# A planned order of the matmul steps in a fused attention and GEGLU kernel

## The chip, the cores and the metric

The kernel runs on one NeuronCore of a Trainium2 chip. The metric is the device time of one execution in microseconds (us). A core has five engines with a queue each, worked off in order: TensorE (PE; its weight loads are shown as PEld), VectorE (DVE), ScalarE (ACT), GpSimd (POOL) and SyncE (SP), which here only issues DMAs. Matmuls write to eight banks of an accumulator memory, PSUM.

## The reference

The input x has 2048 rows of 576. After a layer norm, two branches are computed from the same rows and multiplied:

```python
xn = _layernorm(x)
# A: 32 heads of width 18
q, k, v = split(xn @ wqkv)
p = softmax(q @ k.T * 18 ** -0.5)
s = concat_heads(p @ v) @ wo
# B: gated MLP, inner width 4608
h = gelu(xn @ w_gate) * (xn @ w_up)
g = silu(h @ w_down)
out = x + s * g
```

All is fp32. The kernel gets near fp32 from fp16 matmuls by splitting operands into a high and a low half (three products for one).

## The kernel before, in words

**Stages.** A first stage (to about 210 us) makes the layer norm, the first projections and the row maxima of head pair 0. Then the main loop (lines 1464 to 1528) goes over head pairs 0 to 14, 64 steps each. A last stage (from line 1544) does pair 15, the output projection and the gating.

**A step of the main loop** issues, in this order: `qk2` (line 1265), the scores of this pair for one key tile, followed by the exponential on ScalarE (L1275, from PSUM tile s2); `qk1` (line 1212), scores of the next pair, followed by their row maxima on VectorE (L1220, from s1); and then one of three fillings. s1 and s2 exist once, so the next step's scores wait for this step's maximum and exponential. The fillings are:
- *gate slots* (`g_run`, line 1001): the GEGLU's first matmuls. `Pair` (line 415) computes a tile of the gate and one of the up product in banks ma and mb at once, with half the array each, in two stages of 14 and 13 slots (L443, two matmuls a slot). At the end of the second, ScalarE empties ma (gs, L608) and mb (gv, L619), and a chain follows on GpSimd (L631 to L634), ScalarE (tanh, L637), GpSimd (L644, L645), ScalarE (hhi, L659) and GpSimd (hlo, L666).
- *a down stage* (`DownPair.run`, line 716): half of a down product, in the two-bank tile md (L729). After the second one VectorE adds md to the sum y (L749, called late in the step).
- *a PV run* (`burst`, line 1300): probabilities by values for the two to four key tiles that are waiting, in one bank, in fp32 (L1310). VectorE then adds the bank to osb (L1316, L1318).

In before, a running account (`stored`) of the work left, spread over the steps left, says how many slots a step gets, and whether a down pair may begin. When a gate pair closes, the next step makes the PV run, in bank ma and, if anything is left, mb.

**Deferred work.** `subtick` (line 141) is called once in each step. It advances a clock of ticks: deferred functions (the chain of a gate pair, the division of finished heads) come due some ticks after they were asked for, if the step has room for them; the room is given to it by engine, in us (A for ScalarE, V for VectorE, T for the step's length, which pays back GpSimd). Behind them comes a background list, `bg`, of pieces that prepare the weights.

**Weights.** Chunks follow each other in the gate stream: projection chunks j1 to j4 (seven heads each) and gate chunks c0 to c17 (256 inner columns each), in the order j1, c0, c1, j2, c2, c3, j3, c4, c5, j4, c6 and so on to c17, then the output weights. `prep` (line 195) prepares one in pieces: load; absolute maxima on VectorE (L234, L239); exchange of the maximum through DRAM (L260, L275); a power-of-two scale (L281 to L298); five times a high half on ScalarE (L316) and a low half on GpSimd (L323, L324); the same for the down weights (L333). A VectorE piece asks for 0.7 of V, a ScalarE piece for 0.7 of A. When the gate stream comes to a chunk, `unit_w` (line 963) calls `until` (line 160), which repeats subticks, with plenty of room, till the last piece of that chunk is issued; then the chunk's first slot is issued.

**Finished heads.** `norm` (line 1323) divides by the row sums. The sums go through DRAM and back in four DMAs (a1, a2, b1, b2), since the reciprocal has to be spread over the rows of each head; the steps are chained by ticks. Only the last one of all (pair 15, second half) does it on VectorE with a shuffle and a reciprocal over all 512 columns (L1335, L1336).

Of the kernel before, what the change touches and what calls it, by code (L numbers as in the profile page):

```python
# [12 lines left out]
F32 = mybir.dt.float32  # L13
F16 = mybir.dt.float16
I32 = mybir.dt.int32
AF = mybir.ActivationFunctionType
# [4 lines left out]
P = 128  # L21
# [75 lines left out]
def kernel(ctx: ExitStack, tc: tile.TileContext, x, wqkv, wo, w_gate, w_up, w_down, out):  # L97
# [1225 lines left out]
    def norm(p, qh, o):  # L1323
        st = {}
        last = p == NPAIR - 1

        def a():
            if o is None:
                st["o"] = osum.pop((p, qh))
                return  # L1330
            st["o"] = ap.tile([P, 512], F32, tag="osb", name=f"osb_{p}_{qh}", bufs=2)
            nc.scalar.activation(st["o"], o, AF.Copy)
            if last and qh == 1:
                st["b"] = ap.tile([P, 512], F32, tag="obr", name=f"obr_{p}_{qh}", bufs=1)
                nc.vector.stream_shuffle(st["b"], st["o"], mask=[DH] * 32)  # L1335
                nc.vector.reciprocal(st["b"], st["b"])  # L1336
                return

        def a1():
            st["sd"] = dp.tile([4, 512], F32, tag="sd", name=f"sd_{p}_{qh}", bufs=2)  # L1340
# [54 lines left out]
            defer.at(defer.now + dt, run, cost)  # L1395

        a()
        if last and qh == 1:
            for fn in (c, d, e, g):
                fn()  # L1400
        else:
            dma = ((1, a1, None), (3, a2, None), (3, b, None), (1, b1, None), (2, b2, None))
            if p < NPAIR - 2:
                chained(*dma, (4, c, on_dve()), (1, d, on_act()), (1, e, on_dve()), (1, f, None))
            else:
                dma = ((1, a1, None), (2, a2, None), (2, b, None), (1, b1, None), (1, b2, None))

                def rest():
                    for fn in (c, d, e, g if last else f):
                        fn()  # L1410

                chained(*dma, (3, rest, on_dve()))
# [33 lines left out]
    zero_last()  # L1446
    pend = []
    dn = None
    stored = 0.0
    gs.closed = False  # L1450
    G_SLOT, D_STAGE = 0.2158, 0.735
    whole = (NPAIR - 1) * 4 * NT
    dleft = 2 * NCH * NT

    def flush(tags):

        for tag in tags:
            if not pend:
                return
            n = next((k + 1 for k, u in enumerate(pend) if u[2] == NT - 1), len(pend))  # L1460
            burst(pend[:n], tag)
            del pend[:n]

    for p in range(NPAIR - 1):
        if p not in VT:
            load_v(p)
        for i in range(4 * NT):
            s, half = divmod(i, 2)
            qh, kt = divmod(s, NT)
            if i == 0:  # L1470
                until(lambda: mdone.get(p))
            if i == 52 and p + 2 < NPAIR:
                load_qk(p + 2)
            kp = p + 1 if s < 30 else p + 2
            if i == 60:
                items = iter(range(64))
            pt = qk2(p, 2 * qh + half, kt, "s2")
            if half == 0:
                pa = pt
            else:  # L1480
                pend.append((p, qh, kt, pa, pt))
            if kp < NPAIR:
                qk1(kp, next(items))
            if i == 62:
                steps[2]()
            stored += (gs.left * G_SLOT + dleft * D_STAGE) / max(1, whole - 64 * p - i)
            late = False
            spent = 0.0
            held = 2 * len(pend) + (half == 0)
            cap = 8 if 64 * p + i < whole - 3 else 6  # L1490
            if dn is None and len(dnq) > 1 and not 58 <= i <= 60 and (gs.closed or held < cap - 2):
                dn = DownPair()
                dn.run()
                spent = D_STAGE
            elif dn is not None:
                late = dn.run()
                spent = D_STAGE
            if spent:
                dleft -= 1
            stored -= spent  # L1500
            if gs.closed:
                gs.closed = False
                if late:
                    dn.evac()
                    dn = None
                k = len(pend)
                subtick({"A": 2.2, "V": 1.4 if late else 2.2, "T": 1.0 + 0.86 * k})
                flush(("ma", "mb"))
            else:
                subtick({"A": 0.75, "V": 0.0 if late else 0.75, "T": 1.85})  # L1510
                if late:
                    dn.evac()
                    dn = None
                r = g_left()
                n = max(stored, (1.8 if late else 1.27) - spent) / G_SLOT
                if n < r:
                    n = math.ceil(r / max(1, round(r / max(n, 1.0))))
                n0 = gs.left
                g_run(n)
                stored -= (n0 - gs.left) * G_SLOT  # L1520
                if held >= cap and not gs.closed:
                    subtick({"A": 1.5, "V": 1.5, "T": 3.0})
                    flush(("md",))
            if i == 60:
                steps[1]()
            if i == 59:
                steps = max_end(p + 1)
                steps[0]()
# [97 lines left out]
```

## Time and profile before

| | us |
|---|---|
| median of 3 runs (lowest to highest) | 2699.47 (2698.98 to 2701.22) |
| the profiled execution's own time | 2701.04 |
| its span, first to last instruction | 2699.0 |

The profile has the span's busy times by engine, groups of instructions by source line (L1310 is line 1310), the waits by pair of engine and releaser, and a timeline. In the timeline a row is: start, busy time, engine, line, operation, output<-inputs, shapes, count, and in brackets the idle time of the engine before it with what ended it. TensorE's work overlaps its weight loads, and its ends are modelled.

### The profile page before, as it was taken

How to read it: one execution, taken by the hardware profiler on the slowest of the kernel's cores; microseconds unless marked ns; L12 is line 12 of the kernel's file. 1: busy time of each engine (PE TensorE's matmuls, PEld its weight loads, DVE VectorE, ACT ScalarE, POOL GpSimd, SP SyncE). 2: the span in 40 equal slices, each digit the busy share in tenths (PEclk: the TensorE clock that was granted, in tenths of full speed). 3: DMA queues.
4: the chain of work that ended last, by engine and by line, in shares of the span. 5: the costliest groups of instructions: out<-in, count | busy, mean ns of one | idle time of the engine just before them, and what ended most of it. 6: DMA issues, size and time to landing. Idle time of an engine off the chain costs nothing.

```text
span 2699.0 us, 59766 instructions
## 1 busy us (share of the span) xinstructions
PE 2556.7 (95%) x25292; PEld 1359.9 (50%) x25292; DVE 1922.6 (71%) x2718; ACT 1655.4 (61%) x2083; POOL 1485.3 (55%) x1422
## 2 busy tenths in 40 slices
PE   6979999999999999999999999999999999999898
PEld 5554545455545544445554545555455555544344
DVE  7677778777777787677767777777777777766534
ACT  5216666666667665666666666767666666666663
POOL 4236663575357553657575665747476675756201
PEclk9989999999999999999999999999999999999999
DMA  4420111201130022011111111111011120100033
GB/s 142 140 80 23 21 38 54 68 17 28 58 82 12 9 53 64 26 38 32 30 28 32 36 28 38 41 24 47 15 32 28 38 54 10 43 14 15 7 103 114
DMA packets 134068, 118.90 MB, mean 44 GB/s; under 512 B 60456, under 2 KB 113088, under 8 KB 133800
## 3 DMA queue, kind: packets, MB, share of 16 engines
q1 hardware_dynamic: 128168, 103.31, 14.7%
q0 software_dynamic: 3072, 8.90, 1.0%
q8 instruction: 197, 3.23, 0.5%
q10 hardware_dynamic: 2560, 2.89, 0.3%
q14 instruction: 71, 0.58, 0.1%
HBM read 85.16 MB, written 29.63 MB: 43 GB/s over the span
## 4 chain that ended last, share of the span: by engine, by line
PE 76%; DVE 11%; ACT 7%; issue 3%; DMA 2%; POOL 0%; SPq 0%; ACTq 0%; DVEq 0%
PE ma_t L443 15%; PE ma_t L1310 15%; PE md_t L729 13%; PE mb_t L443 13%; PE s L1269 7%; PE s L1217 6%; DVE PM L1220 3%; ACT P L1275 3%; ACT gs L608 2%; DVE osb L1318 2%; DVE y L749 2%; PE pv L1291 1%; PE mc_t L462 1%; PE mb_t L1310 1%; ACT hhi L659 1%
## 5 line engine op out<-in xcount | busy, mean ns | idle before, releaser
L1220 DVE TENSOR_REDUCE PM<-s 128x2 f32<-128x1024 f32 x1024 | 1251.5, 1223 | 349.6 <-PE s L1217 345.4
L1275 ACT ACTIVATE P<-s,etab 128x1024 f32<-128x1024 f32 x896 | 996.9, 1113 | 738.5 <-PE s L1269 728.4
L443 PE MATMUL ma_t<-XHT,whi_c 64*128 64x512 f16 x1440 | 541.2, 376 | 22.6 <-DVE osb L1318 18.9
L443 PE MATMUL mb_t<-XHT,whi_c 64*128 64x512 f16 x1440 | 542.0, 376 | 3.2 <-DVE touch L413 1.2
L443 PE MATMUL ma_t<-XHT,wlo_c 64*128 64x512 f16 x1296 | 487.0, 376 | 0.0
L1310 PE MATMUL ma_t<-P,VT 128*32 128x512 f32 x3624 | 421.6, 597 | 38.7 <-ACT gs L608 29.3
L443 PE MATMUL mb_t<-XL,whi_c 64*128 64x512 f16 x1152 | 433.0, 376 | 0.0
L443 PE MATMUL mb_t<-XHT,wlo_c 64*128 64x512 f16 x1152 | 432.9, 376 | 0.0
L443 PE MATMUL ma_t<-XL,whi_c 64*128 64x512 f16 x1152 | 432.9, 376 | 0.0
L1269 PE MATMUL s<-QT,KT 56*128 56x512 f16 x2048 | 408.2, 380 | 14.5 <-ACT P L1275 10.7
L443 PEld LDWEIGHTS <-whi_c 64*128 64x128 f16 x5184 | 289.6, 94 | 252.6 <-issue 51.8
L1217 PE MATMUL s<-KT,QT 54*128 54x512 f16 x2048 | 408.2, 379 | 5.9 <-DVE PM L1220 3.3
L644 POOL TENSOR_SCALAR tw<-tw 128x512 f32<-128x512 f32 x144 | 88.9, 618 | 522.2 <-ACT tw L637 522.2
L729 PE MATMUL md_t<-dhi_c,hhi 64*128 64x288 f16 x2264 | 340.6, 283 | 7.5 <-DVE touch L413 4.2
L729 PE MATMUL md_t<-dhi_c,hlo 64*128 64x288 f16 x2264 | 340.4, 282 | 0.0
L729 PE MATMUL md_t<-dlo_c,hhi 64*128 64x288 f16 x2264 | 339.9, 282 | 0.0
L729 PEld LDWEIGHTS <-hhi 64*128 64x128 f16 x4528 | 249.4, 94 | 138.9 <-issue 34.7
L666 POOL TENSOR_TENSOR hlo<-gv,hhi 128x512 f16<-128x512 f32 x144 | 168.6, 1171 | 198.9 <-ACT hhi L659 198.9
L1269 PEld LDWEIGHTS <-KT 56*128 56x128 f16 x2048 | 129.2, 94 | 281.7 <-issue 193.9
L1318 DVE TENSOR_TENSOR osb<-ma_t,osb 128x512 f32<-128x512 f32 x142 | 98.0, 690 | 209.3 <-PE ma_t L1310 209.3
L1310 PEld LDWEIGHTS ma_t<-P,VT 128*32 128x32 f32 x3624 | 103.1, 109 | 261.8 <-issue 190.7
L631 POOL TENSOR_TENSOR tw<-gs 128x512 f32<-128x512 f32 x144 | 150.1, 1043 | 120.0 <-ACT gs L608 119.2
(261 smaller groups left out, 4071.5 us busy)
## 6 DMA issues: line engine op xcount, KB each, us to landing
draw_c<-in_B_w_down SPq DMA_DIRECT2D x18, 576.0 KB
raw_c<-in_B_w_gate SPq DMA_DIRECT2D x18, 512.0 KB
raw_c<-in_B_w_up SPq DMA_DIRECT2D x18, 512.0 KB
obr<-rd SPq DMA_DIRECT2D x31, 256.0 KB
KT<-KD SPq DMA_DIRECT2D x32, 224.0 KB
QT<-QD SPq DMA_DIRECT2D x32, 216.0 KB
VS<-vst POOLq DMA_DIRECT2D x16, 304.0 KB, 3.8
VT<-VS SPq DMA_DIRECT2D x16, 304.0 KB
```

The lines of the kernel that those rows point to most:

```text
L443: nc.tensor.matmul(o, lw, xx, start=self.stage == 0 and self.k == 0, stop=self.stage == 1 and self.k == self.slots - 1, skip_group_check=True,
L608: nc.scalar.activation(st["g"], g.t, AF.Copy, scale=w.uE[:, 0:1])
L631: gp.tensor_tensor(st["t"], st["g"], st["g"], op=ALU.mult)
L644: gp.tensor_scalar(st["t"], st["t"], 1.0, 1.0, op0=ALU.mult, op1=ALU.add)
L666: gp.tensor_tensor(hs.lo[:, ft], st["v"], hs.hi[:, ft], op=ALU.subtract)
L729: nc.tensor.matmul(self.t.t[:, hf, 0:288], a[r, ft, sl], b[r, ft, 288 * hf:288 * hf + 288], start=self.stage == 0 and k == 0, stop=self.st ...
L1217: nc.tensor.matmul(s1[:, h], QT[p][r, P * qt:P * qt + P], KT[p][r, 512 * kb:512 * kb + 512], start=True, stop=True)
L1220: nc.vector.tensor_reduce(PM[p][:, :, qt, kb:kb + 1], s1, op=ALU.max, axis=AX.X)
L1269: nc.tensor.matmul(s2[:, h], KT[p][r, P * kt:P * kt + P], QT[p][r, 512 * qb:512 * qb + 512], start=True, stop=True)
L1275: nc.scalar.activation(pt, s2, AF.Exp, scale=ETAB[j0])
L1310: nc.tensor.matmul(t.t[qd:qd + 32, :], VT[p][:, c0:c0 + 32], pt[:, h], start=kt == k0, stop=kt == k1, skip_group_check=True,)
L1318: nc.vector.tensor_tensor(osum[p, qh], t.t, osum[p, qh], op=ALU.add)
```

## The change

- **A plan for each gate pair.** When a pair has closed and its PV run is issued, `make_plan` tries every pattern of the next 4 to 7 steps: which of them have a down stage, where the pair's first stage ends, and how the 14 and 13 slots are shared out (`spread`). The pattern with the least modelled loss (`lost`, which follows TensorE and the row maxima with fixed times) is taken, with small penalties for a length or a number of down stages off the average. The account `stored` is gone. The last step of a plan makes the PV run.
- **Room for VectorE.** In a step that isn't a run, V was 0.75 unless a down pair ended there. Now it is 0.75 only if also the step's planned work (0.735 for a down stage and 0.2158 a slot) is 2.0 or more. In a run step it stays 2.2 (1.4 where a down pair ends).
- **The run's bank.** With a down stage in the step, ma and mb as before; without one, md, and ma for a second run.
- **The end.** The plan spreads the work over the steps left and LEAD = 10 more, so that some gate slots and down pairs fall into the last stage. By the order of instructions, 40 slots do, and 18 single down products in place of 10.
- **One norm.** Pair 14's second half takes the way without DRAM, too.

```diff
--- before.py
+++ after.py
@@ -1324,17 +1324,18 @@
         st = {}
         last = p == NPAIR - 1
 
+        direct = qh == 1 and p >= NPAIR - 2
+
         def a():
             if o is None:
                 st["o"] = osum.pop((p, qh))
-                return
-            st["o"] = ap.tile([P, 512], F32, tag="osb", name=f"osb_{p}_{qh}", bufs=2)
-            nc.scalar.activation(st["o"], o, AF.Copy)
-            if last and qh == 1:
+            else:
+                st["o"] = ap.tile([P, 512], F32, tag="osb", name=f"osb_{p}_{qh}", bufs=2)
+                nc.scalar.activation(st["o"], o, AF.Copy)
+            if direct:
                 st["b"] = ap.tile([P, 512], F32, tag="obr", name=f"obr_{p}_{qh}", bufs=1)
                 nc.vector.stream_shuffle(st["b"], st["o"], mask=[DH] * 32)
                 nc.vector.reciprocal(st["b"], st["b"])
-                return
 
         def a1():
             st["sd"] = dp.tile([4, 512], F32, tag="sd", name=f"sd_{p}_{qh}", bufs=2)
@@ -1395,8 +1396,8 @@
             defer.at(defer.now + dt, run, cost)
 
         a()
-        if last and qh == 1:
-            for fn in (c, d, e, g):
+        if direct:
+            for fn in (c, d, e, g if last else f):
                 fn()
         else:
             dma = ((1, a1, None), (3, a2, None), (3, b, None), (1, b1, None), (2, b2, None))
@@ -1446,11 +1447,80 @@
     zero_last()
     pend = []
     dn = None
-    stored = 0.0
     gs.closed = False
-    G_SLOT, D_STAGE = 0.2158, 0.735
+    G_SLOT, D_STAGE, BLOCK, BURST = 0.2158, 0.735, 0.43, 2.9
+    ROW_MAX, EVAC, ADD, TOUCH = 1.28, 0.86, 0.75, 0.15
+    LEAD = 10
     whole = (NPAIR - 1) * 4 * NT
-    dleft = 2 * NCH * NT
+    dleft = [2 * NCH * NT]
+    plan = deque()
+    frac = [0.0, 0.0]
+
+    def spread(total, ds, lates):
+
+        n = len(ds)
+        base = (total * G_SLOT + sum(ds) * D_STAGE - 0.4 * sum(lates)) / n
+        left, out = total, []
+        for k in range(n):
+            w = base + 0.4 * lates[k] - ds[k] * D_STAGE
+            m = left if k == n - 1 else min(left, max(0, round(w / G_SLOT)))
+            out.append(m)
+            left -= m
+        return out
+
+    def lost(steps):
+
+        t = vec = red = 0.0
+        ideal = 0.0
+        for d, g, late, first in steps:
+            t1 = max(t + 0.21, red + 0.055)
+            e1 = t1 + 0.22
+            vec = red = max(vec, e1 + 0.16) + ROW_MAX - 0.05
+            w = d * D_STAGE + (BURST if g is None else g * G_SLOT)
+            if d:
+                vec = max(vec, e1 + D_STAGE) + (EVAC if late else TOUCH)
+            t = e1 + w
+            if g is None:
+                vec = max(vec, t) + ADD
+            elif first:
+                vec = max(vec, t) + TOUCH
+            ideal += BLOCK + w
+        return max(t, red + 0.055 - 0.21) - ideal
+
+    def make_plan(now, held, mid, avail):
+
+        pairs = max(1.0, gs.left / 27)
+        size = (whole + LEAD - now) / pairs + frac[0]
+        want = min(8.0, dleft[0] / pairs + frac[1])
+        best = None
+        for n in range(max(4, math.floor(size) - 1), min(9 - held, 7, math.ceil(size) + 1) + 1):
+            for bits in range(1 << n):
+                ds = [bits >> k & 1 for k in range(n)]
+                lates, run, ok, starts = [], mid, True, 0
+                if mid and not ds[0]:
+                    continue
+                for k, d in enumerate(ds):
+                    lates.append(bool(d and run))
+                    if d and not run:
+                        starts += 1
+                        at = now + k
+                        ok = ok and not 58 <= at % 64 <= 60 and at < whole - 1 and starts <= avail
+                    if run and not d:
+                        ok = False
+                    run = bool(d) and not run
+                if not ok:
+                    continue
+                for m in range(1, n - 1):
+                    gl = spread(14, ds[:m], lates[:m]) + spread(13, ds[m:n - 1], lates[m:n - 1]) + [None]
+                    seq = [(d, g, l, k == m - 1) for k, (d, g, l) in enumerate(zip(ds, gl, lates))]
+                    works = [d * D_STAGE + g * G_SLOT for d, g, _, _ in seq[:-1]]
+                    cost = lost(seq) + 0.3 * abs(n - size) + 0.15 * abs(sum(ds) - want) + 0.02 * (max(works) - min(works))
+                    if best is None or cost < best[0]:
+                        best = (cost, seq, works + [9.0])
+        _, seq, works = best
+        frac[0] = max(-1.5, min(1.5, size - len(seq)))
+        frac[1] = want - sum(d for d, _, _, _ in seq)
+        return [(d, g, w) for (d, g, _, _), w in zip(seq, works)]
 
     def flush(tags):
 
@@ -1483,44 +1553,34 @@
                 qk1(kp, next(items))
             if i == 62:
                 steps[2]()
-            stored += (gs.left * G_SLOT + dleft * D_STAGE) / max(1, whole - 64 * p - i)
+            now = 64 * p + i
+            held = 2 * len(pend) + (half == 0)
+            if not plan and gs.pair is None and not gs.closed:
+                plan.extend(make_plan(now, held, dn is not None, len(dnq) // 2))
+            step = plan.popleft() if plan else None
             late = False
-            spent = 0.0
-            held = 2 * len(pend) + (half == 0)
-            cap = 8 if 64 * p + i < whole - 3 else 6
-            if dn is None and len(dnq) > 1 and not 58 <= i <= 60 and (gs.closed or held < cap - 2):
-                dn = DownPair()
-                dn.run()
-                spent = D_STAGE
-            elif dn is not None:
+            if step is None:
+                d = dn is not None or len(dnq) > 1 and not 58 <= i <= 60 and held < 6
+            else:
+                d = step[0]
+            if d:
+                if dn is None:
+                    dn = DownPair()
                 late = dn.run()
-                spent = D_STAGE
-            if spent:
-                dleft -= 1
-            stored -= spent
+                dleft[0] -= 1
             if gs.closed:
                 gs.closed = False
                 if late:
                     dn.evac()
                     dn = None
-                k = len(pend)
-                subtick({"A": 2.2, "V": 1.4 if late else 2.2, "T": 1.0 + 0.86 * k})
-                flush(("ma", "mb"))
+                subtick({"A": 2.2, "V": 1.4 if late else 2.2, "T": 1.0 + 0.86 * len(pend)})
+                flush(("ma", "mb") if d else ("md", "ma"))
             else:
-                subtick({"A": 0.75, "V": 0.0 if late else 0.75, "T": 1.85})
+                subtick({"A": 0.75, "V": 0.0 if late or step is None or step[2] < 2.0 else 0.75, "T": 1.85})
                 if late:
                     dn.evac()
                     dn = None
-                r = g_left()
-                n = max(stored, (1.8 if late else 1.27) - spent) / G_SLOT
-                if n < r:
-                    n = math.ceil(r / max(1, round(r / max(n, 1.0))))
-                n0 = gs.left
-                g_run(n)
-                stored -= (n0 - gs.left) * G_SLOT
-                if held >= cap and not gs.closed:
-                    subtick({"A": 1.5, "V": 1.5, "T": 3.0})
-                    flush(("md",))
+                g_run(7 if step is None else step[1])
             if i == 60:
                 steps[1]()
             if i == 59:
```

## The prediction

> **What bounds the kernel now.** I read the page's busy table and clock row first, then a table of windows by stage, then the groups and the waits of the main loop, then the timeline at single places.
>
> ```profile
> PE 2556.7 (95%) x25292; PEld 1359.9 (50%) x25292; DVE 1922.6 (71%) x2718; ACT 1655.4 (61%) x2083; POOL 1485.3 (55%) x1422
> PEclk9989999999999999999999999999999999999999
> ```
> ```profile
> 210.00:2531.00 2321.00, 2240.07 (x22762) 1173.59 (x22762) 1706.37 (x2356) 1501.16 (x1862) 1397.83 (x1294) 1.00 0.14 34
> 2531.00:2546.00 15.00, 10.61 (x61) 3.96 (x60) 3.66 (x8) 8.62 (x11) 3.09 (x4) 0.77 0.01 3
> 2546.00:2571.00 25.00, 18.17 (x114) 6.18 (x113) 10.07 (x18) 18.13 (x21) 0.00 (x0) 0.96 0.21 56
> ```
>
> In the windows the columns are length, then busy time of PE, PEld, DVE, ACT and POOL, the granted clock, DMA share and GB/s. The main loop (210 to 2546) is nine tenths of the time, and TensorE is busy in it for 2240 of 2321 us at full clock. The change takes no matmul out: by the built programs' order of instructions, before has 173 PV runs and after 174, and gate slots and down stages are the same in number. So it can win only the time in which TensorE stands still, and lose by making it stand still longer. These rows say what it waits for (after the second bar: idle time before the group, and what ended it):
>
> ```profile
> L1310 PE MATMUL ma_t<-P,VT 128*32 128x512 f32 x3624 | 421.6, 597 | 38.7 <-ACT gs L608 29.3 <-DVE evl L494 8.9
> L1310 PEld LDWEIGHTS ma_t<-P,VT 128*32 128x32 f32 x3624 | 103.1, 109 | 261.8 <-issue 190.7 <-ACT gs L608 57.6 <-DVE evl L494 13.0
> L749 DVE SCALAR_TENSOR_TENSOR y<-md_t,c_c,y 128x576 f32<-128x576 f32 x267 | 215.1, 806 | 0.0
> ```
> ```profile
> PE ma_t L443 <- DVE osb L1318: 20.6, 67, 1.7
> ...
> PE s L1269 <- ACT P L1275: 10.7, 15, 1.9
> ```
>
> A PV run writes bank ma right after a gate pair closed there, and waits until ScalarE has emptied it (gs). After the run the next gate pair waits until VectorE has added it up (osb).
>
> **The change part by part.** *PV runs in md.* With no down stage in the closing step the run now goes to md, which nobody has to empty first. By the order, 81 steps of before begin their run in ma without a down stage, and 97 of after in md. The wait for gs and evl lies between 38.7 (PE) and 57.6 + 13.0 = 70.6 (its weight loads, which begin to wait some 0.2 us before the array runs dry; about 100 of them, so 70.6 - 20 = 50). I take 50. Back comes the wait of a run that follows a second down stage: 32 of the 97, whose y (0.81) must leave md, at an estimated 0.25 each, 8. **-42**; ends -71 and -15.
>
> *The bank after the run.* Before, 77 ma runs were followed by a gate slot in the same bank (20.6/67 = 0.31 us each). After, 57 md runs are followed by a down stage in md and 6 by a gate slot in the bank of the run: 63 x 0.31 = 19.5. The wait moves. **-3**; ends -12 and +7.
>
> *Gate work kept for the last heads.* The end of the main loop and the start of the last stage are thin now:
>
> ```profile
> 2532.61 0.24 PE L1239 MATMUL md_t<-ident,rmc 128*64 128x128 f16 x1 [0.98 <-DVE rmc L1233]
> 2535.22 0.61 PE L1269 MATMUL s<-QT,KT 56*128 56x512 f16 x2 [1.94 <-ACT P L1275]
> 2537.03 0.61 PE L1269 MATMUL s<-QT,KT 56*128 56x512 f16 x2 [1.20 <-ACT P L1275]
> ```
> ```profile
> 2567.34 0.39 PE L1269 MATMUL s<-QT,KT 56*128 56x512 f16 x2 [0.99 <-ACT P L1275]
> 2570.73 0.42 PE L462 MATMUL ma_t<-whi_wo,ohl 128*128 128x288 f16 x1 [3.00 <-DMA ohl<-OHL]
> ```
> ```profile
> 2568.90:2575.60 6.70, 4.87 (x20) 1.60 (x21) 0.00 (x0) 1.62 (x3) 0.00 (x0) 0.51 0.76 223
> ```
>
> Work put there fills idle time of 0.98 + 1.94 + 1.20 = 4.1, and of a clock of 0.77 over 15 us another 3.4: **-7.5**; ends -10 and 0. At the handoff some 6 us idle (3.00 and three waits of 0.99) and half of 6.7 - 1.6 us at half clock go: -8.6. But in after's order four of the five low halves of the output weights are issued only at the first output product:
>
> ```profile
> L323 POOL TENSOR_SCALAR raw_wo<-raw_wo,s_wo 128x576 f32<-128x576 f32 x5 | 9.1, 1811 | 0.0
> L324 POOL TENSOR_TENSOR wlo_wo<-raw_wo,whi_wo 128x576 f16<-128x576 f32 x5 | 6.4, 1279 | 0.4
> ```
>
> 4 x 3.09 = 12.4, against 1.7 us in which 14 products reach the last: +10.6. Together **+2**; ends -9 and +11.
>
> *One norm without DRAM.* Four DMAs become a shuffle and a reciprocal on VectorE:
>
> ```profile
> L1336 DVE RECIPROCAL obr<-obr 128x512 f32<-128x512 f32 x1 | 3.4, 3354 | 0.0
> ```
>
> They stand after VectorE's last row maximum, where no score waits for it: **0**; ends -3 and +3 (the length of that DMA wait).
>
> *The plan.* Steps of 3 slots beside a down stage, the shortest, fall from 193 to 131. But steps whose planned work is under 2.0 us now give VectorE's background pieces no room (before: 0.75 in nearly every step). They bunch in the run steps: by the order, steps with over 2.5 us of such work rise from 25 to 59. **0**; ends -20 and +15.
>
> *What that does to the weights.* This is the term that decides. The pieces that prepare a chunk's weights (maxima, scale, split into high and low half) are paced by that room. When the gate stream reaches a chunk whose pieces aren't all issued, the program issues the rest at once, with every deferred step of the last gate pair, and only then the chunk's first matmul. Before, the order has this once in the main loop, at chunk c1 (two last pieces). After has it at 18 switches. The one of before can be read:
>
> ```profile
> 294.63 1.44 ACT L333 ACTIVATE dhi_c<-draw_c,s_c 128x576 f16<-128x576 f32 x2
> 297.24 0.39 PE L1269 MATMUL s<-QT,KT 56*128 56x512 f16 x2
> 298.75 0.62 ACT L637 ACTIVATE tw<-tw 128x512 f32<-128x512 f32 x1
> 299.50 0.38 PE L1269 MATMUL s<-QT,KT 56*128 56x512 f16 x2
> 300.16 1.26 POOL L645 TENSOR_TENSOR gv<-gv,tw 128x512 f32<-128x512 f32 x1
> 301.45 0.63 ACT L659 ACTIVATE hhi<-gv 128x512 f16<-128x512 f32 x1 [2.08 <-POOL gv L645]
> 301.99 1.10 ACT L1275 ACTIVATE P<-s,etab 128x1024 f32<-128x1024 f32 x1
> 303.13 0.39 PE L1269 MATMUL s<-QT,KT 56*128 56x512 f16 x2 [1.60 <-ACT P L1275]
> ```
> ```profile
> L666 POOL TENSOR_TENSOR hlo<-gv,hhi 128x512 f16<-128x512 f32 x144 | 168.6, 1171 | 198.9 <-ACT hhi L659 198.9
> L323 POOL TENSOR_SCALAR raw_c<-raw_c,s_c 128x512 f32<-128x512 f32 x90 | 141.2, 1568 | 64.2 <-ACT whi_c L316 64.1
> L324 POOL TENSOR_TENSOR wlo_c<-raw_c,whi_c 128x512 f16<-128x512 f32 x90 | 104.2, 1158 | 7.5
> ```
>
> The step starts at 297.24. ScalarE's queue holds tanh, then hhi, which waits 2.08 us for GpSimd, then the next exponential: TensorE is released 5.89 us after the start and has lost 1.60. A step of one down stage and five slots took 2.26 (297.24 to 299.50), so scores cost about 0.44, a down stage 0.74, a slot 0.215. In after the steps behind a switch are mostly down + 4, 6 and 4 slots: the third starts at 2.05 + 2.48 = 4.5, the last slot of the first half pair, which reads the last low half, at 6.35. Two splits of down weights (1.44) now stand ahead of the exponential: 5.89 + 1.44 = 7.3, so 2.8 lost. On GpSimd hhi (ends at 4.84) is followed by hlo (6.0) and the missing low halves at 1.57 + 1.16 = 2.73 each, ending at 8.8, 11.5, 14.2:
> - one or none missing (c7, c9, c13, c14, c10, c16): the exponential decides, about 3.1 each (steps of 3 to 6 slots), 19;
> - two (c3, c5, c8, c11, c12): 11.5 - 6.35 = 5.2 each, 26;
> - three (c1, c15, c17): 14.2 - 6.35 = 7.9 each, less the 1.60 of before, 22;
> - j3, smaller, without down weights: 2.3;
> - all five (c2, c4, c6, behind projection chunks): from the first split to the last low half the trace of c0 has 153.19 to 167.92:
>
> ```profile
> 153.19 0.72 ACT L316 ACTIVATE whi_c<-raw_c,s_c 128x512 f16<-128x512 f32 x1 [8.94 <-DVE s_c L298]
> ...
> 166.77 1.15 POOL L324 TENSOR_TENSOR wlo_c<-raw_c,whi_c 128x512 f16<-128x512 f32 x1
> ```
>
> That is 14.7. Ahead of it on VectorE stand the add of the run, the row maximum and the scale's five small instructions:
>
> ```profile
> L1220 DVE TENSOR_REDUCE PM<-s 128x2 f32<-128x1024 f32 x1024 | 1251.5, 1223 | 349.6 <-PE s L1217 345.4
> L1318 DVE TENSOR_TENSOR osb<-ma_t,osb 128x512 f32<-128x512 f32 x142 | 98.0, 690 | 209.3 <-PE ma_t L1310 209.3
> L281 DVE TENSOR_REDUCE mg_c<-mb_c 128x2 f32<-128x256 f32 x18 | 7.3, 407 | 0.6 <-DMA mb_c<-mxd_c 0.6
> L298 DVE TENSOR_SCALAR s_c<-s_c 128x2 f32<-128x2 f32 x18 | 8.1, 451 | 0.6
> ```
>
> 0.69 + 1.22 + five of 0.15 to 0.45 each (2.0 with the gaps between them) put the first split at an estimated 3.9 after the step's start, so the last half ends at 18.6; TensorE wants it at 4.25: 14.4 each, and c6 has two DMAs more (4, near the one wait of 3.00 above): 47.
>
> **+117** in all. The next chunk's weight load waits on SyncE's queue until GpSimd has let go of the raw tile, and the head loads and norm DMAs behind it wait too; they are due many steps later, so I cost that at nothing (it belongs to rival 3). The low end is 18 stalls like the one seen, 29 less 1.6; the high end 160, if VectorE's forced norm steps (all four DMAs of one at c1 and c3) come on top.
>
> *The clock.* It halves after idling (the window at 0.51 follows 3.00 and 0.99 us; the one at 0.77 holds 4.1), losing about (6.7 - 1.6)/2 = 2.5 each time. Eight to eleven of the stalls are as long: 8 x 2.5, **+20**; ends 0 and +45. The Trainium skill (TensorE: Matmul & The Clock Gate, Part 1: The HAM clock gate) has the gate fall to half after an idle window of about 3.4 us; the trace halves at 3.00 and less. By the page only the eight longest stalls count, by the rows all 18, which would be 45.
>
> **Sum.** -42 - 3 - 7.5 + 2 + 0 + 0 + 117 + 20 = +86.5, on the profiled execution's own 2701.04 (span 2699.0 and 2.0 around it): 2787.5. The median of the runs is 1.6 lower: **2786 us**.
>
> **The rivals.**
> 1. *Faster: the forced pieces stay cheap.* If ScalarE and GpSimd run far enough ahead, each switch costs what the seen one cost: 27 for 117, no clock: 2699.5 - 50.5 + 27 = 2676. It decides from a mean of 2.8 us a switch (50.5/18). For it: the only example lost 1.60. Against: there no low half was missing, and GpSimd can't start one before its scale and high half exist.
> 2. *The run's wait only changes its bank:* VectorE's fuller run steps hold y and the adds up, so the first two terms give -15 and +7 and the rest stands: 2786 + 37 = 2823.
> 3. *Every switch halves the clock and the norm's DMAs come on top:* 2786 + 25 + 43 = 2854.
>
> **Chances.** Forecast 0.62, rival 1 0.13, rival 2 0.15, rival 3 0.10. The range leaves out rival 1 and half of rival 3; its low end takes a switch cost near 65 (2734) with the better first term: 2725 to 2850. A measurement tells 0.2% (5 us) from no change: faster 0.13, same 0.02, slower 0.85.
>
> **What would show it.** In after's profile: the idle time before L1310 down by some 40; waits of PE or its weight loads for wlo (POOL), which no row of before has, of 15 us three times; the wait of L1269 for ACT P up from 10.7 to over 40; tenths under 9 in PE's row and under full in the clock row at the switches; a wait for wlo_wo at the first output product. I am wrong if POOL finished the low halves before the first slots needed them, or if those waits sum to under 50 us.

## The result, and the profile after

The changed kernel takes **2845.36 us** (median of 4 runs, 2839.47 to 2851.53) against 2700.16 of before (4 runs, 2698.98 to 2701.22): a ratio of 1.0538, interval 1.0511 to 1.0565. It is 145 us slower. The forecast was 2786 with a range of 2725 to 2850: right in direction, 59 us short.

The page of after, busy times and the rows in 40 slices for TensorE and its granted clock:

```profile
PE 2596.4 (91%) x25244; PEld 1341.8 (47%) x25244; DVE 1939.7 (68%) x2721; ACT 1666.3 (58%) x2083; POOL 1492.1 (52%) x1422
...
PE   6989898889979998899899999889999989989888
...
PEclk9989999999999999899999999999999999999999
```

TensorE's row was nearly all 9; now an 8 stands in every second or third slice. It issues no more matmuls than before (x25244 against x25292) and is yet busy 40 us longer. The main loop and what follows it, by windows (columns as in the prediction):

```profile
205.00:2644.00 2439.00, 2258.88 (x22574) 1143.95 (x22572) 1714.03 (x2344) 1503.76 (x1849) 1373.82 (x1269) 0.97 0.13 33
2644.00:2722.00 78.00, 52.89 (x402) 23.32 (x399) 26.32 (x43) 37.82 (x49) 38.60 (x34) 0.91 0.07 17
```

The loop's clock was 1.00 and is 0.97, and TensorE stands still for 180 us of it, where before left 81 of its 2321. The groups of after say what it waits for:

```profile
L443 PE MATMUL ma_t<-XHT,whi_c 64*128 64x512 f16 x1440 | 553.0, 384 | 29.0 <-ACT whi_c L316 19.2
L443 PE MATMUL ma_t<-XHT,wlo_c 64*128 64x512 f16 x1296 | 500.3, 386 | 50.1 <-POOL wlo_c L324 50.0
...
L729 PE MATMUL md_t<-dhi_c,hhi 64*128 64x288 f16 x2232 | 336.1, 288 | 21.4 <-DVE osb L1318 19.3
...
L1310 PE MATMUL md_t<-P,VT 128*32 128x512 f32 x2224 | 259.2, 597 | 0.4 <-ACT rms L1241 0.3
```
```profile
PEld L443 <- POOL wlo_c L324: 68.9, 25, 8.5
...
PE s L1269 <- ACT P L1275: 54.5, 16, 6.9
...
ACT hhi L659 <- POOL gv L645: 37.5, 15, 3.0
```

The wait that the new bank was for is gone: 38.7 us before L1310, now 0.4. New are waits for the weights: 50.0 for low halves, 19.2 for high ones, and 54.5 for the exponential where before had 10.7. Nearly all of this falls on the 18 late switches, where the gate stream comes to a chunk whose weight pieces aren't all issued. One of them in full, at chunk c8 (timeline of after):

```profile
1396.18 0.40 PE L1269 MATMUL s<-QT,KT 56*128 56x512 f16 x2
...
1398.44 0.38 PE L443 MATMUL ma_t<-XHT,whi_c 64*128 64x512 f16 x1
...
1399.31 0.63 ACT L637 ACTIVATE tw<-tw 128x512 f32<-128x512 f32 x1 [3.32 <-POOL tw L633]
...
1401.16 1.57 POOL L645 TENSOR_TENSOR gv<-gv,tw 128x512 f32<-128x512 f32 x1
...
1402.77 0.63 ACT L659 ACTIVATE hhi<-gv 128x512 f16<-128x512 f32 x1 [2.31 <-POOL gv L645]
...
1403.30 1.43 ACT L333 ACTIVATE dhi_c<-draw_c,s_c 128x576 f16<-128x576 f32 x2
...
1404.63 1.09 ACT L1275 ACTIVATE P<-s,etab 128x1024 f32<-128x1024 f32 x1
1405.78 0.61 PE L1269 MATMUL s<-QT,KT 56*128 56x512 f16 x2 [6.95 <-ACT P L1275]
```

Read it from the bottom. The scores at 1405.78 wait for the exponential at 1404.63, whose own scores were written at 1396.18. ScalarE takes it eight microseconds later, since ahead of it in its queue stand the tanh of the last gate pair, which waits for GpSimd, then hhi, which waits for GpSimd again, and then two splits of down weights. All of it was put there at once by `until`. The array runs dry with its last gate slot (1398.44) and stands for 6.95 us. TensorE then runs its next matmuls at half clock (0.61 where 0.39 is usual):

```profile
1404.00:1406.00 2.00, 0.22 (x2) 0.13 (x3) 0.61 (x1) 1.73 (x3) 2.00 (x2) 0.50 0.08 18
1406.00:1410.00 4.00, 3.54 (x22) 1.59 (x18) 1.37 (x2) 1.11 (x1) 3.83 (x4) 0.50 0.00 0
1410.00:1414.00 4.00, 3.75 (x46) 2.31 (x48) 2.72 (x4) 1.90 (x2) 3.92 (x4) 0.97 0.55 158
```

### The profile page after: what moved, and what is told of

Its sections match the earlier page's. It is cut to its first block, busy times and chain, and to the rows that moved or that the text cites. A ratio compares the mean times of both kernels' runs of the same rounds, so it can differ in the third digit from the quotient of the medians.

```text
span 2849.8 us, 59614 instructions
## 1 busy us (share of the span) xinstructions
PE 2596.4 (91%) x25244; PEld 1341.8 (47%) x25244; DVE 1939.7 (68%) x2721; ACT 1666.3 (58%) x2083; POOL 1492.1 (52%) x1422
## 4 chain that ended last, share of the span: by engine, by line
PE 69%; POOL 9%; DVE 8%; issue 7%; ACT 4%; DMA 3%; SPq 0%; ACTq 0%; POOLq 0%; DVEq 0%
PE mb_t L443 14%; PE ma_t L443 13%; PE md_t L729 12%; PE s L1269 7%; PE s L1217 6%; PE md_t L1310 6%; PE ma_t L1310 5%; POOL raw_c L323 3%; DVE PM L1220 2%; POOL wlo_c L324 2%; ACT P L1275 1%; DVE osb L1318 1%; PE pv L1291 1%; POOL gv L645 1%; DMA obr<-rd 1%
## 5 line engine op out<-in xcount | busy, mean ns | idle before, releaser
L443 PE MATMUL ma_t<-XHT,whi_c 64*128 64x512 f16 x1440 | 553.0, 384 | 29.0 <-ACT whi_c L316 19.2
L443 PE MATMUL mb_t<-XHT,whi_c 64*128 64x512 f16 x1440 | 552.9, 384 | 3.6 <-ACT gv L619 2.3
L443 PE MATMUL ma_t<-XHT,wlo_c 64*128 64x512 f16 x1296 | 500.3, 386 | 50.1 <-POOL wlo_c L324 50.0
L1269 PE MATMUL s<-QT,KT 56*128 56x512 f16 x2048 | 409.7, 388 | 68.4 <-ACT P L1275 54.5
L443 PE MATMUL mb_t<-XHT,wlo_c 64*128 64x512 f16 x1152 | 443.1, 385 | 0.0
L443 PE MATMUL ma_t<-XL,whi_c 64*128 64x512 f16 x1152 | 442.2, 384 | 0.0
L443 PE MATMUL mb_t<-XL,whi_c 64*128 64x512 f16 x1152 | 442.2, 384 | 0.0
L1217 PE MATMUL s<-KT,QT 54*128 54x512 f16 x2048 | 412.2, 387 | 12.8 <-DVE PM L1220 7.7
L443 PEld LDWEIGHTS <-whi_c 64*128 64x128 f16 x5184 | 282.1, 95 | 257.1 <-issue 36.5
L729 PE MATMUL md_t<-dhi_c,hhi 64*128 64x288 f16 x2232 | 336.1, 288 | 21.4 <-DVE osb L1318 19.3
L729 PE MATMUL md_t<-dhi_c,hlo 64*128 64x288 f16 x2232 | 335.5, 287 | 0.0
L729 PE MATMUL md_t<-dlo_c,hhi 64*128 64x288 f16 x2232 | 335.4, 286 | 0.0
L729 PEld LDWEIGHTS <-hhi 64*128 64x128 f16 x4464 | 244.3, 95 | 166.2 <-issue 51.9
L1310 PE MATMUL md_t<-P,VT 128*32 128x512 f32 x2224 | 259.2, 597 | 0.4 <-ACT rms L1241 0.3
L323 POOL TENSOR_SCALAR raw_c<-raw_c,s_c 128x512 f32<-128x512 f32 x90 | 143.3, 1592 | 191.0 <-ACT whi_c L316 128.9
L443 PEld LDWEIGHTS <-wlo_c 64*128 64x128 f16 x2592 | 141.9, 95 | 188.4 <-POOL wlo_c L324 68.9
```

What stands on the lines that cost most here:

```text
L323: nc.gpsimd.tensor_scalar(raw, raw, sc, None, op0=ALU.mult)
L443: nc.tensor.matmul(o, lw, xx, start=self.stage == 0 and self.k == 0, stop=self.stage == 1 and self.k == self.slots - 1, skip_group_check=True,
L729: nc.tensor.matmul(self.t.t[:, hf, 0:288], a[r, ft, sl], b[r, ft, 288 * hf:288 * hf + 288], start=self.stage == 0 and k == 0, stop=self.st ...
L1217: nc.tensor.matmul(s1[:, h], QT[p][r, P * qt:P * qt + P], KT[p][r, 512 * kb:512 * kb + 512], start=True, stop=True)
L1269: nc.tensor.matmul(s2[:, h], KT[p][r, P * kt:P * kt + P], QT[p][r, 512 * qb:512 * qb + 512], start=True, stop=True)
L1310: nc.tensor.matmul(t.t[qd:qd + 32, :], VT[p][:, c0:c0 + 32], pt[:, h], start=kt == k0, stop=kt == k1, skip_group_check=True,)
```

## The experiments

The theory is that of the prediction: the rule for VectorE's room makes the weights late, and all else is a net gain. Three rivals are tested, with numbers of their own: the plan itself costs the time (1); the run's new bank only moves its wait (2); the late weights cost only their idle time and the clock nothing (3). A ratio is against runs of before on the same chip.

**The rule taken back, all else of the change kept (e1_room).**

```diff
-subtick({"A": 0.75, "V": 0.0 if late or step is None or step[2] < 2.0 else 0.75, "T": 1.85})
+subtick({"A": 0.75, "V": 0.0 if late else 0.75, "T": 1.85})
```

> The changed kernel with one thing put back: VectorE's room is 0.75 again in every step in which no down pair ends, as before. By the order of instructions only two switches then issue pieces late, c1 (no low half missing) and c2 (one). Theory (late weights cost all that was lost): the prediction's other terms stay, 2700 - 42 - 3 - 7.5 - 8.6 = 2639, between 2610 and 2665, and no wait of PE for wlo over a few us. Rival (the plan or the bank of the PV run costs it): still over 2780. Rival (half and half, the clock falling for other reasons): 2700 to 2780.

Measured: 2657.62, ratio 0.9844 (0.9827 to 0.9861). The rule costs 188 us, and without it the change is a gain of 42. Page and groups of this kernel:

```profile
PE 2536.9 (96%) x25232; PEld 1332.3 (50%) x25232; DVE 1923.6 (73%) x2720; ACT 1662.7 (63%) x2083; POOL 1492.3 (56%) x1422
...
L729 PE MATMUL md_t<-dhi_c,hhi 64*128 64x288 f16 x2224 | 330.4, 283 | 14.8 <-DVE osb L1318 12.4 <-DVE osb L1316 1.9 <-DVE y L749 0.3
...
L1310 PE MATMUL md_t<-P,VT 128*32 128x512 f32 x2232 | 260.0, 596 | 0.5 <-DVE y L749 0.3
```

No wait for a low half is left. TensorE's busy time falls by 59.5 us (2596.4 - 2536.9) with the same work, and the granted clock rises from 0.960 to 0.992. The two profiled executions are 199 us apart, so three tenths of the rule's cost are slower matmuls and the rest is idle time.

**The rule alone in before's order (e3_starved_before).** The step's work is counted before the subtick, and V is 0 where it is under 2.0; no plan, no new bank.

```diff
-subtick({"A": 0.75, "V": 0.0 if late else 0.75, "T": 1.85})
...
+work = spent + min(n, r) * G_SLOT
+subtick({"A": 0.75, "V": 0.0 if late or work < 2.0 else 0.75, "T": 1.85})
```

> The kernel before with the room rule of the change alone: a step whose planned work is under 2.0 us gives VectorE's deferred pieces no room. No plan, no md, no LEAD. By the order of instructions 17 switches then issue pieces late, with low halves missing at 12 of them: five at c2, c4, c6, three at c14, two at c1, c9, c17, one at six more. Theory (late weights): by the changed kernel's own stalls, 188 us for 18 switches with 34 low halves missing (with the run that put the room back), some 150 us here: 2800 to 2880. Rival (the plan is needed for the harm): within 40 us of 2698.

Measured: 2864.13, ratio 1.0611 (1.0595 to 1.0627), +164 us without a plan anywhere. Rival 1 falls as the cause. Two groups of this kernel:

```profile
L443 PE MATMUL ma_t<-XHT,wlo_c 64*128 64x512 f16 x1296 | 499.9, 386 | 39.4 <-POOL wlo_c L324 39.4
L1269 PE MATMUL s<-QT,KT 56*128 56x512 f16 x2048 | 414.9, 387 | 70.1 <-ACT P L1275 58.6
```

The same two waits, of about the same size, in another order of the steps.

**After, with the stalls filled (e9_warm).** At each of the 18 late switches TensorE gets 10 matmuls of 128x128x512 more, and 8 more for each low half not yet issued, into a tile that nobody reads. Everything else stays.

```diff
...
 def unit_w(i):
     start_prep(i)
+    miss = -1 if preps[i].ready else 5 - preps[i].nlo
     until(lambda: preps[i].ready)
+    if miss >= 0 and blocks[0] > 128:
+        spin(10 + 8 * miss)
```

> The changed kernel with work added: at each of the 18 late switches 10 matmuls of 128x128x512, and 8 more for each low half that is missing, are issued ahead of the chunk's first slot into the tile s1; nobody reads them (108 us of TensorE work in all at full clock). Theory (the stalls cost twice: idle time, and half clock behind it, about 60 us of slower matmuls): the added work fills idle time and keeps the clock up, so the time falls, to 2790 to 2835, and the half-clock time in the main loop falls from 167 us to under 100. Rival (the half clock lies in the idle time and costs little): 2845 or more, up to 2890 where the added work overruns the stalls.

Measured: 2821.26, ratio 1.0448 (1.0427 to 1.0469); clock 0.986 against 0.960. Its busy times:

```profile
PE 2660.5 (94%) x25744; PEld 1371.5 (49%) x25744; DVE 1937.4 (69%) x2721; ACT 1666.6 (59%) x2083; POOL 1491.8 (53%) x1422
```

500 matmuls more, which follow each other every 0.216 us, are 108 us of work; the kernel is 24 us faster for it. TensorE is busy for only 64 us more than in after, so all its other matmuls together take 44 less. So TensorE had that time to spare at the switches, and part of what a switch costs comes after it, through the clock. Rival 3 falls.

**The pieces let free, the rule kept (e5_prep_free).** VectorE's weight pieces ask for no room; deferred work still obeys the rule.

```diff
-act, dve = on_act(), on_dve()
+act, dve = on_act(), None
```

> The changed kernel, its room rule kept, but VectorE's pieces of the weights' preparation ask for no room (the norms' pieces still do). By the order no switch issues anything late. Theory (late weights): as fast as the run with the room put back, within 20 us, near 2640. Rival (the rule's harm is in the crowded run steps on VectorE, or in the late norms): 2760 to 2845, since the pieces are then issued in the first steps there are, up to three a step.

Measured: 2684.32, ratio 0.9942 (0.9926 to 0.9959). That is 161 us off after, so it is the pieces that the rule starves. But it is 27 us more than e1, where at most 20 were expected. A group of this kernel, to be held against the same one of e1:

```profile
L729 PE MATMUL md_t<-dhi_c,hhi 64*128 64x288 f16 x2224 | 331.5, 283 | 29.6 <-DVE osb L1318 17.6 <-DVE y L749 10.5 <-DVE osb L1316 0.8
```

VectorE empties md and adds the runs later here: 29.6 against 14.8 before L729, and PV runs wait 6.9 us for y to leave md (0.3 in e1). That is 21 of the 27. That it comes from pieces which crowd into one step, with no room asked, is argued and not shown. Pacing them has its use; the rule's amount was wrong.

**The run's bank, undone and done alone (e4_room_ma, e2_md_only).** e4 is e1 with the old banks; e2 is before with nothing but the new banks.

```diff
 e4_room_ma
-flush(("ma", "mb") if d else ("md", "ma"))
+flush(("ma", "mb"))
 e2_md_only
-flush(("ma", "mb"))
+flush(("ma", "mb") if spent else ("md", "ma"))
```

> As the run with the room put back, but every PV run goes to ma and mb, as before, so that the bank is told from the plan. Theory: about 42 us more than that run, 2670 to 2695, with some 40 us of idle time before L1310 again. Rival (the plan's spacing alone brings the gain): within 10 us of it.

> The kernel before with one part of the change alone: a PV run without a down stage in its step goes to md (then ma). No plan, LEAD or norm. Theory: the wait for gs and evl before the run goes (42 to 50), the wait for osb after it moves or shrinks: 2650 to 2662, with the idle time before L1310 near 0. Rival (the wait only changes its bank): within 15 us of 2700.

Measured: e4 2681.27, ratio 0.9934 (0.9917 to 0.9952); e2 **2636.03**, ratio 0.9770 (0.9755 to 0.9785). Within the plan the bank is worth 24 us (42 were expected), alone in before's order 62 (38 to 50 were expected). And e4, with the plan, the later end and the norm but the old banks, is 17 us under before: these and the bank gain something each, but together (e1) less than the bank alone. A group of e4, and three of e2:

```profile
L1310 PE MATMUL ma_t<-P,VT 128*32 128x512 f32 x3528 | 412.5, 599 | 46.0 <-ACT gs L608 38.0 <-DVE evl L494 7.9
```
```profile
L443 PE MATMUL ma_t<-XHT,whi_c 64*128 64x512 f16 x1440 | 541.1, 376 | 4.7 <-DVE osb L1316 2.7 <-DVE evl L494 1.5 <-ACT gs L608 0.6
...
L729 PE MATMUL md_t<-dhi_c,hhi 64*128 64x288 f16 x2264 | 335.2, 283 | 8.0 <-DVE touch L413 4.0 <-DVE y L749 3.2 <-DVE osb L1316 0.3
...
L1310 PE MATMUL md_t<-P,VT 128*32 128x512 f32 x1928 | 228.6, 600 | 1.3 <-DVE y L749 1.3
```

In before's order a gate slot, in ma, mostly follows the run. With the run in md it waits neither for gs nor for osb: both waits go, the one of L443 for osb down to 2.7 from 20.6. The plan mostly puts a down stage, in md, right behind the run, and so keeps the second wait (12.4 in e1). Rival 2 holds for that one wait, in the plan only.

**The norm without DRAM, undone and done alone (e7_room_dram, e8_md_norm).** e7 is e1 with the DRAM way for pair 14; e8 is e2 with the direct way for it.

```diff
 e7_room_dram
-direct = qh == 1 and p >= NPAIR - 2
+direct = qh == 1 and last
```

> The run with the room put back, with pair 14's second half divided through DRAM again. Theory (the reciprocal of 3.4 us stands ahead of the down products' sums on VectorE, and the split behind it ahead of the exponential on ScalarE, while PE waits): 6 to 14 us less, 2643 to 2652 against 2657. Rival (with gate work left in the last stage VectorE's queue holds nothing that PE waits for): within 4 us of 2657.

> The kernel before with two parts of the change: the PV runs in md, and pair 14's second half divided on VectorE without DRAM. Theory: the wait for the output rows at the handoff (3.1 us in the run with md alone) goes, with the half clock behind it (up to 3): 2630 to 2636 against 2636. Rival (the rows come late whichever way, since their stores stand behind others on SyncE's queue): no change, 2634 to 2640, with the wait still over 2 us.

Measured: e7 2647.69, ratio 0.9816 (0.9803 to 0.9830), 10 us better than e1 (8 by the ratios); e8 2647.92, ratio 0.9806 (0.9791 to 0.9821), 12 us worse than e2 and 9 worse than its repeat below. The expectation for e8 was wrong. Rows of e8's timeline at the handoff, from the main loop to the output projection, and one from behind it:

```profile
2479.83 3.35 DVE L1338 RECIPROCAL obr<-obr 128x512 f32<-128x512 f32 x1
...
2483.94 0.63 ACT L1364 ACTIVATE onh<-osb 128x512 f16<-128x512 f32 x1 [9.00 <-DVE osb L1360]
...
2485.21 0.51 DVE L698 SCALAR_TENSOR_TENSOR y<-ma_t,c_c,y 128x288 f32<-128x288 f32 x1
...
2485.78 0.40 PE L691 MATMUL ma_t<-dhi_c,hhi 128*128 128x288 f16 x1 [5.29 <-DVE y L698]
...
2488.49 0.56 SPq L1209 DMA_DIRECT2D VT<-VS  x1
...
2492.44 1.93 PE L1291 MATMUL pv<-P,VT 128*32 128x512 f32 x8 [3.08 <-DMA VT<-VS]
...
2567.36 0.42 PE L844 MATMUL mb_t<-wodh,onh 64*128 64x288 f16 x1 [6.17 <-ACT onh L1364]
```

The reciprocal over 512 columns takes 3.35 us, but the price is what stands behind it. ScalarE's next instruction in order, onh, waits 9.00 us at the head of its queue, and with it the exponentials and whatever has to be emptied from PSUM; the banks of the down products are added to y only after it (L698), and the load of VT follows ten stores of the normed heads on SyncE's queue. TensorE stands still for 5.29, 3.08 and, at pair 15's first half, 6.17 us, where e2 has one wait of 3.12 for the output rows and 0.90 at the last place; what delays pair 15's rows was not traced. In after the same wait (7.15 us before onh at 2663.75) holds back gs, and the next gate pair waits for it:

```profile
2663.75 0.63 ACT L1364 ACTIVATE onh<-osb 128x512 f16<-128x512 f32 x1 [7.15 <-DVE osb L1360]
...
2665.94 0.67 ACT L608 ACTIVATE gs<-ma_t,uE_c 128x512 f32<-128x512 f32 x1
...
2666.67 0.58 PE L443 MATMUL ma_t<-XHT,whi_c 64*128 64x512 f16 x1 [5.24 <-ACT gs L608]
```

TensorE's wait for gs at this place is 4.58 us in e1 and, with the DRAM way, 0.63 in e7.

**The plan's other rules (e12_plan_md, e10_plan_lead2).** e12 is e1 with a plan that never begins with a down stage unless one is open, so that a gate slot follows the run. e10 is e12 with the DRAM norm and less work kept for the end.

```diff
 e12_plan_md, e10_plan_lead2
-if mid and not ds[0]:
+if mid != bool(ds[0]):
 e10_plan_lead2
-LEAD = 10
+LEAD = 2
```

> The run with the room put back, with one rule more in the plan: the first step behind a PV run has no down stage, unless a down pair is under way. Theory (the plan doesn't know that the run's bank md has to be added up before a down stage may write it: 14.8 us of idle time before L729, 12.7 before the scores for late row maxima): 8 to 15 us less than that run, 2640 to 2650. Rival (the order of the steps matters little; the plan loses at the handoff alone, where two gate pairs follow each other without a run between): within 5 us of 2657.

> What is left of the plan at its best: room put back, no down stage first behind a run, pair 14 through DRAM, and LEAD = 2 in place of 10, so that hardly any gate work is left for the last stage. Theory (LEAD's two gate pairs without a run between them cost some 7 us of idle time at the handoff, the norm some 10): 2630 to 2645, about as the md runs alone (2636). Rival (the plan's spacing itself is worth 10 us or more): under 2626. Rival (it costs as much): over 2650.

Measured: e12 2654.42, ratio 0.9833 (0.9817 to 0.9849), not told apart from e1; e10 2655.13, ratio 0.9841 (0.9828 to 0.9854), 7 us worse than e7. Both theories fell. With the rule of e12 more runs fall into steps with a down stage and go to ma, and the wait for osb moves to the gate slot behind them instead of going away: the 12.4 us before L729 in e1 became this row.

```profile
PE ma_t L443 <- DVE osb L1318: 13.4, 48, 0.5
```

LEAD = 2 shortens the handoff, but by leaving the work in the loop: from the last row-maximum scores to the first output product e10 needs 44.8 us against 59.5 in e7, while TensorE's idle time in it only falls from 8.1 to 6.5. Its time is over 2650, as the rival had it by which the plan's spacing costs time.

**The bank alone once more, on the same chip as e7 and e10 (e2_again).**

> The kernel before with the PV runs in md alone, again, on the same chip as the two runs beside it, so that they can be told from it: 2630 to 2642.

Measured: 2639.21, ratio 0.9777 (0.9764 to 0.9791). Before with the run in md and nothing else is the fastest version found, 58 to 62 us under before and 206 under after. The plan, even with room and the DRAM norm (e7), is 8.5 us behind it. Loops of e7 and e2_again, by windows:

```profile
205.00:2460.00 2255.00, 2200.33 (x22480) 1135.19 (x22482) 1693.85 (x2341) 1501.37 (x1851) 1384.72 (x1275) 1.00 0.14 35
```
```profile
205.00:2460.00 2255.00, 2222.49 (x22726) 1143.98 (x22722) 1705.10 (x2352) 1498.42 (x1861) 1394.31 (x1290) 1.00 0.14 35
```

Both are at full clock; in the same stretch TensorE stands still 55 us with the plan and 33 without.

## Why the prediction was right in direction and 59 us short

| step of the prediction | forecast | the runs |
|---|---|---|
| PV runs in md | -42 (-71 to -15) | -24 in the plan (e4 to e1), -62 alone with the bank behind the run (e2) |
| the bank after the run | -3 | waits of L729 for osb: 19.3 in after (forecast 19.5); in before's order (e2) the wait goes |
| end of the loop and handoff | -5.5 | about +13 of idle time, the norm's part in it |
| one norm without DRAM | 0 (-3 to +3) | +8 to +10 (e7), +9 to +12 (e8) |
| the plan | 0 (-20 to +15) | about +8 beside the bank (e7 against e2_again); about -17 with the old banks, LEAD and the norm in it (e4) |
| late weights | +117 | about 116 of idle time at the switches |
| the clock | +20 (0 to 45) | about +60 |

In two lumps: the rule for the room cost 188 us where 117 + 20 and the 10.6 for late output weights make 148, and the rest of the change brought 42 where -42, -3, -7.5 and -8.6 make 61. Of the 59 us, 40 are in the first and 19 in the second.

**Late weights: right in place; in the sum partly by luck.** The stalls of 1.8 us and more at the 18 switches add up to about 116 us in after's trace, and those of 1 us and more to 129. (The prediction's own list adds up to 116.3, not 117.) By class it was less exact, and the errors cancel: one or no low half missing 26 (forecast 19), two 34 (26), three 23.4 (22 + the 1.60 of before), j3 5.2 (2.3); but behind the projection chunks c2, c4 and c6 only 27.5 instead of 47, since there the slots ran one by one between a low half and the next, at half clock. In the class with two missing the path was another, too: it was to be the second low half on GpSimd, but all five stalls (5.29 to 6.95 us) ended with the exponential, as at c8 above. Only c1, c15 and c17 waited for low halves as forecast. Of the signs that it named, the sum of the waits for wlo (50.0 for TensorE, 68.9 for its weight loads), the exponential's 54.5 us and the tenths under 9 in PE's row came. Three waits of 15 us did not (the longest for wlo took 8.5), the clock row shows the switches in one slice only, and the first output product waited for ohl and not for wlo_wo.

**The clock: the step that failed.** The prediction took 2.5 us for the eight longest stalls, 20 in all, with a high end of 45. But TensorE's busy time alone, at the same work, is 59.5 us longer than without the rule, which is 3.3 for each of 18. Two things were mis-sized. The number: half clock follows 17 of the 18 switches, and it doesn't take a long stall. In after's trace the clock changes on a grid of 3.41 us. Here are three windows of that grid at full clock, each with the one after it. The first holds a stall of 2.37 us (ended at 1122.47). The second holds 1.34 us of one of 2.17 (ended at 834.18) and nearly all of one of 1.51 before it. The third holds 1.90 us of the stall at c16, of 2.26 (ended at 2431.14):

```profile
1120.07:1123.48 3.41, 1.04 (x12) 0.71 (x11) 3.41 (x5) 0.98 (x1) 0.00 (x0) 1.00 0.08 25
1123.48:1126.89 3.41, 3.41 (x20) 1.92 (x17) 1.30 (x2) 1.11 (x1) 0.00 (x0) 0.50 0.24 67
...
829.93:833.35 3.42, 0.61 (x4) 0.11 (x4) 1.01 (x1) 0.89 (x2) 3.25 (x4) 1.00 0.00 0
833.35:836.76 3.41, 2.58 (x14) 0.92 (x16) 1.22 (x2) 1.27 (x2) 3.33 (x3) 0.50 0.38 114
...
2427.37:2430.78 3.41, 1.51 (x20) 0.94 (x18) 1.34 (x3) 1.33 (x3) 3.24 (x3) 1.00 0.05 7
2430.78:2434.20 3.42, 3.06 (x34) 1.91 (x35) 2.10 (x3) 1.52 (x3) 3.34 (x4) 1.00 0.72 182
```

TensorE is idle for 2.37, 2.81 and 1.90 us of the three, and half clock follows the first two only. So what counts is the idle time in one window, not the length of one stall. It holds for the whole main loop of after: 20 windows at full clock have 2.24 us of idle time or more, and half clock follows each; the other 645 have 1.91 or less, and it follows none. Over the main loops of all runs half clock follows every window with more than 1.91 us of idle time and none with less than 1.73; between the two, both occur.

And the length: where TensorE goes on with gaps, the clock stays down. At c2 and c6 it is at half for 17.1 and 27.3 us; in the second stretch TensorE's 12.75 busy us all lie behind the end of the stall, at 1145.40:

```profile
1137.13:1164.44 27.31, 12.75 (x56) 3.33 (x58) 7.73 (x15) 8.39 (x12) 18.49 (x13) 0.50 0.22 66
...
495.00:513.00 18.00, 11.72 (x56) 3.11 (x54) 3.94 (x5) 6.94 (x9) 17.50 (x13) 0.53 0.17 50
```

The Trainium skill (TensorE: Matmul & The Clock Gate, Part 1: The HAM clock gate) has a window of 3413 ns that runs freely, and sums it up as no idle times over about 3.4 us. The trace agrees with the window: its stretches at half clock in the main loop last 3.41, 6.83, 10.24 us and so on up to 27.31. It doesn't agree with the sum-up, which took the short stalls out of the forecast: 2.24 us of idle time in a window were enough. The prediction had a row at 3.00 and should have gone by its rows: its own figure for all 18 was 45, still 15 too low. e9 shows that the clock is a cause and not a mere companion.

**The handoff: wrong sign.** From the last row-maximum scores to the first output product before needs 40.7 us, after 77.2. Most of the difference is work that now runs there: TensorE is busy for 52.1 us of it, where before had 28.9. Its idle time is 25.1 against 11.8, so +13 where -7.5 - 8.6 + 10.6 = -5.5 was forecast; the mean clock is about the same (0.91 and 0.90). With the rule taken back (e1) the idle time is 11.3, in e7 8.1: so the work moved there saves less than was forecast, too. Two things are visible in after. One is the norm, above. The other is the output weights:

```profile
2715.94 1.27 POOL L324 TENSOR_TENSOR wlo_wo<-raw_wo,whi_wo 128x576 f16<-128x576 f32 x1
2717.24 0.40 SPq L857 DMA_DIRECT2D ohl<-OHL  x1
2721.83 1.81 PEld L462 LDWEIGHTS <-ohl 128*128 128x128 f16 x9 [12.97 <-DMA ohl<-OHL]
2721.84 0.42 PE L462 MATMUL ma_t<-whi_wo,ohl 128*128 128x288 f16 x1 [12.68 <-DMA ohl<-OHL]
```

The forecast let the first products begin and wait for the last low half. But the tile of the heads' outputs (ohl, tag "raw", lines 848 to 857) takes the buffer of raw_wo, so its load goes out only 0.03 us after the last low half has read it, and takes another 4.6 us: 12.68 idle in place of 10.6, at the end of a chain over GpSimd, SyncE's queue and the DMA.

**Norm and plan at nothing: the norm was wrong.** The prediction named where the reciprocal stands (after the last row maximum) but not who is queued behind it: ScalarE's onh. It asked what stands behind a late weight load on SyncE's queue, but not what stands behind this on ScalarE's. The plan was within its ends.

**The rivals.** *The forced pieces stay cheap* fell: a switch cost about 6.5 us idle (116/18), above its 2.8. *The run's wait only changes its bank* fell for the wait on gs, and held for osb (19.3 us). *Every switch halves the clock* was right in its first half, and too dear in the second (norm DMAs on top): it gave 2854, nearer than the forecast, for one reason out of two.

**What stays open.** Why the plan, with room and the DRAM way, is still some 8 us behind before's simple account. The waits say where it loses: e7 waits 12.4 us before L729 for osb and 12.9 before L1217 for row maxima, e2_again waits 0.3 and 3.9 at these places. At the handoff the plan is ahead (8.1 us idle at full clock, against 11.6 at 0.86). But e12 only moved the wait for osb and e10 did not help, so what in the plan would have to change isn't shown.

## What to carry to other kernels

When a program paces background work by room, a change to the room is a change to every deadline behind it: list the places where the program forces what is late, and price each by the longest in-order queue there, then add the clock for every stall that leaves a large part of a clock window idle, and not only the longest. When an operation is moved off a slow path (here four DMAs), look at who is queued behind its consumer, not only at its own time. And try the parts of a change apart: one line of this one was worth 62 us, and another cost 188.

## What the runs showed of the hardware that was not expected

- Half clock followed a 3.41 us window in which TensorE was idle for 2.24 us or more, made up of several stalls or one; a stall of 2.26 us that two windows shared (1.90 in the first) was followed by none. While TensorE worked with gaps (busy for 11.72 of 18 us at c2, and for 12.75 of the 19.04 us behind the stall of c6) the clock stayed at half, for up to 27.3 us in one piece.
- Idle TensorE time could be bought back with work for nothing: 500 needless matmuls, about 108 us of them, made the kernel 24 us faster (e9_warm).
